# Opening of an attention and token-mixing kernel: which 512 KB tiles the one DMA queue fetches first, and what the first chunks of h wait for

## The chip, the cores and the metric

One core of a Trainium2 chip runs the whole kernel in one launch. The metric is the device time of the launch in microseconds (us), the median of several runs. Times inside the kernel come from one profiled execution and are counted from the start of its span. TensorE is called PE, VectorE DVE, ScalarE ACT, GpSimd POOL, and SyncE, which issues almost all the DMAs here, SP.

## The reference

The input `x` has 2048 tokens of 1024 channels. A modulation vector is made from one condition row, two residual blocks follow:

```
mod = (silu(c) @ w_mod) split in six rows sa, ca, ga, sb, cb, gb   # 1024 each
h   = layernorm(x) * (1 + ca) + sa
x   = x + ga * attention(h)       # 32 heads of 32, four segments of 512 tokens:
                                  # causal softmax inside a segment, plus a linear memory over the earlier ones
h   = layernorm(x) * (1 + cb) + sb
x   = x + gb * mixer(h)           # MLP across the 2048 tokens, 3584 wide, gelu
```

What matters here is the beginning: the scale row `1 + ca` and the shift row `sa` are needed before the first h exists, and h of the first segment (512 tokens) before any query, key or value.

## The kernel before

All matrix products of the large stages are made from two-part operands: a value is split into a rounded high part (ACT or DVE casts it) and a low part (the difference, by DVE or POOL), `split` at L118, and three products high-high, high-low, low-high are summed. In the opening, everything passes through these steps:

- **Loads.** One queue, on SP, issues tile loads of 512 KB in program order: four scale tiles (`fetch_scale(0)`, L309; tiles `wms0` to `wms3`), the four token tiles `x0` to `x3` of the first segment (L310), four more scale tiles (`fetch_scale(1)`, L311), then, inside the loop of L332, eight shift tiles `wm0` to `wm7`, with the three weight parts of head group 0 (v part 0, q part 0, v part 1) behind the first three. The tiles `wms` and `wm` share eleven buffers.
- **Scale.** The row `ca` is made in two halves of 512 channels. `scale_row(cb)` (L293) multiplies the silu of the condition, one column for each of eight steps, with four loaded tiles and adds up one row in PSUM; `scale_columns(cb, ...)` (L301) copies the row, turns it into four columns by PE, one per chunk of 128 channels, and adds 1. The first half serves chunks 0 to 3, the second chunks 4 to 7.
- **Shift.** Here the weights lie transposed, so a DVE instruction (L335) multiplies a tile `wm` of chunk ct with the broadcast condition `scb` and sums along the row: one column of `sa` per chunk.
- **Normalization.** `norm_all` (L214) takes statistics of the four token tiles on DVE, a few tiny steps, and then normalizes two tiles on ACT (L236) and two on DVE (L234).
- **Chunks of h.** For each of eight chunks, `h_chunk` (L244) has PE transpose four blocks (L247, into one of two PSUM banks), ACT apply scale and shift (L249), ACT cast the high part and DVE make the low part. `first_chunk` (L315) then multiplies the chunk with the weights of head group 0 into three PSUM banks: twelve products for key and value (L195), three for the query (L203).

After chunk 7 the second segment's token tiles are treated in the same way (`seg_load(1)`, `seg_chunks`, with the high part on DVE and every second low part on POOL), the first group's keys, values and queries are copied out of PSUM by ACT (L401, L402, L407) and stacked by small DMAs into operands for the scores. Then 32 iterations of attention run: two passes, eight head groups, two segments each. At the beginning of the second pass the pages of h are loaded anew from DRAM (`reload_h`, L360). During the attention, 32 tiles of the other modulation rows are loaded (`mod_fetch`, L572) into the same three buffers as the raw weights. Behind it come the output projection and the mixer, whose products are made by a seven-product recursion.

Who comes first on an engine is not written out by hand. A scheduler walks through the program, keeps a simulated clock for each engine and the queue, and places, of the instructions whose inputs would be ready, the one that stands first in the program (those under `tc.high_priority()`, as in `scale_row` and `norm_all`, before others). The result is a fixed order for each engine, in which every instruction waits for its own inputs and all behind it wait with it. `tc.issue_after(i)` adds one constraint: what is under it is placed after `i`. In the kernel before, `h_chunk` stands under `tc.issue_after` of the second scale row's last product (L337). A change in the opening can so change the order of later instructions as well.

Of the kernel before, what the change touches and what calls it, by code (L numbers as in the profile page):

```python
# [7 lines left out]
F32 = mybir.dt.float32  # L8
# [4 lines left out]
ALU = mybir.AluOpType  # L13
# [4 lines left out]
S, D, H, DH, F = 2048, 1024, 32, 32, 3584  # L18
P = 128
# [25 lines left out]
def attention_and_mlp(ctx, tc, x, wq, wkv, wo, beta, w1, b1, w2, b2, c, wm_a, wm_b, out):  # L45
    nc = tc.nc
    V, A, G, T, SY = nc.vector, nc.scalar, nc.gpsimd, nc.tensor, nc.sync
# [18 lines left out]
    scb, gaw = (a.tile([P, D], F32, name=n) for n in ("scb", "gaw"))  # L66
# [8 lines left out]
    def bank(tag, bufs, name):  # L75
        return psum.tile([P, 512], F32, tag=tag, bufs=bufs, name=name)
# [35 lines left out]
    saca = acst.tile([P, NK, 2], F32, name="saca")  # L112
# [5 lines left out]
    def split(dst, src, hi_eng, lo_eng):  # L118

        hi, lo = dst[:, 0], dst[:, 1]  # L120
        if hi_eng is A:
            last_hi[0] = A.copy(hi, src)  # L122
        else:
            hi_eng.tensor_copy(hi, src)
        return lo_eng.tensor_tensor(lo, src, hi.bitcast(F32), op=ALU.subtract)  # L125
# [18 lines left out]
    def new_page(name):  # L144
        return page.tile([P, 2, 512], F32R, tag="page", bufs=16, name=name)
# [5 lines left out]
    def fetch_part(g, kind, part):  # L151
        r = a.tile([P, D], F32, tag="raw", bufs=3, name=f"raw{kind}{g}_{part}")
        SY.dma_start(r, (wkv if kind == "v" else wq)[g, :, 1024 * part:1024 * part + 1024])
        return r

    def split_part(g, kind, part, r):

        for i in range(2):
            w = aw.tile([P, 2, 512], F32R, tag="w", bufs=8, name=f"w{kind}0_{g}_{part}_{i}")
            split(w, r[:, 512 * i:512 * i + 512], A, V)  # L160
            W[0, g][kind, 2 * part + i] = w

    def load_part(g, pr, kind, part, res):

        if pr == 0:
            split_part(g, kind, part, fetch_part(g, kind, part))
            return
        for i in range(2):
            w = aw.tile([P, 2, 512], F32R, tag="w", bufs=8, name=f"w{kind}{pr}_{g}_{part}_{i}")
            SY.dma_start(w.bitcast(F32), wsp[g, 2 * part + i if kind == "v" else 4 + i])  # L170
            res[kind, 2 * part + i] = w
# [13 lines left out]
    W = {}  # L185
# [23 lines left out]
    def load_x(pool, tt):  # L209
        t = pool.tile([P, D], F32, tag="x", bufs=XB, name=f"x{tt}")  # L210
        SY.dma_start(t, x[P * tt:P * tt + P])
        return t

    def norm_all(tiles):  # L214

        with tc.high_priority():
            flat = csb.rearrange("p a k -> p (a k)")
            r, t = flat[:, 8:12], flat[:, 12:16]
            nb = t
            mv = flat[:, 0:8].rearrange("p (i a) -> p i a", a=2)  # L220
            for k, src in enumerate(tiles):
                st = const.tile([P, 2, 6], F32, tag="st", bufs=4, name="st")
                for i in range(2):
                    V.bn_stats(st[:, i], src[:, 512 * i:512 * i + 512])
                last_stats = V.bn_aggr(mv[:, k], st)
            A.activation(r, mv[:, :, 1], AF.Ln, bias=eps)
            exp = A.activation(r, r, AF.Exp, scale=-0.5)
            V.scalar_tensor_tensor(t, mv[:, :, 1], EPS, r, op0=ALU.add, op1=ALU.mult)
            V.scalar_tensor_tensor(t, t, -0.5, r, op0=ALU.mult, op1=ALU.mult)
            V.scalar_tensor_tensor(r, t, 1.5, r, op0=ALU.add, op1=ALU.mult)  # L230
            V.scalar_tensor_tensor(nb, mv[:, :, 0], -1.0, r, op0=ALU.mult, op1=ALU.mult)
            for k, src in enumerate(tiles):
                if k % 2:
                    last_v = V.tensor_scalar(src, src, r[:, k:k + 1], nb[:, k:k + 1], op0=ALU.mult, op1=ALU.add)  # L234
                else:
                    last_a = A.activation(src, src, AF.Identity, scale=r[:, k:k + 1], bias=nb[:, k:k + 1])  # L236
        return last_stats, exp, last_a, last_v
# [6 lines left out]
    def h_chunk(pool, xs, seg, ct):  # L244
        ps = bank(*(("s1", 2), ("s2", 2))[ct % 2] if seg else ("s2", 2), f"hps{seg}_{ct}")
        for i in range(4):
            T.transpose(ps[:, 128 * i:128 * i + 128], xs[i][:, P * ct:P * ct + P], ident)  # L247
        h32 = pool.tile([P, L], F32, tag="h32", bufs=HB, name=f"h32_{seg}_{ct}")
        act = A.activation(h32, ps, AF.Identity, scale=saca[:, ct, 1:2], bias=saca[:, ct, 0:1])  # L249
        pg = new_page(f"h{seg}_{ct}")  # L250
        lo = split(pg, h32, V if seg else A, V if ct % 2 or not seg else G)
        hpages[seg, ct] = pg
        return act, lo
# [26 lines left out]
    s1p = left.__enter__()  # L280
    scale_wm = []

    def fetch_scale(cb):
        for i in range(4 * cb, 4 * cb + 4):
            t = s1p.tile([P, 2, 512], F32, tag="wm", bufs=11, name=f"wms{i}")
            SY.dma_start(t.rearrange("p a n -> p (a n)"), wm_a[1, i])
            scale_wm.append(t)
# [5 lines left out]
    def scale_row(cb):  # L293
        ps = bank(*(("ms", 1), ("s1", 2))[cb], f"srow{cb}")
        with tc.high_priority():
            for k in range(NK):
                mm = T.matmul(ps[0:1], sc[:, k:k + 1], scale_wm[4 * cb + k // 2][:, k % 2], start=(k == 0),
                              stop=(k == NK - 1))
        return ps, mm

    def scale_columns(cb, ps):  # L301
# [4 lines left out]
                     skip_group_check=True)  # L306
        V.tensor_scalar_add(saca[:, 4 * cb:4 * cb + 4, 1], scale_ps[:, 4 * cb:4 * cb + 4], 1.0)

    fetch_scale(0)  # L309
    xs = {0: [load_x(s1p, tt) for tt in range(4)]}  # L310
    fetch_scale(1)  # L311
    W[0, 0] = {}
    first = [bank("pj", 2, "nps0_0"), bank("pj", 2, "nps0_1"), bank("s1", 2, "qps0")]

    def first_chunk(ct):  # L315
        h = hpages[0, ct]
        for half in range(2):
            kv_chunk(W[0, 0], h, half, ct, two_tiles(first[half]))
        q_chunk(W[0, 0], h, ct, first[2])

    srow = [scale_row(0)]
    V.tensor_copy(bc, sc.unsqueeze(2).to_broadcast([P, NK, P]))
    for i in range(2):
# [1 line left out]
        for j in range(4):  # L325
            T.transpose(ps[:, 128 * j:128 * j + 128], bc[:, 4 * i + j], ident)
        A.copy(scb[:, 512 * i:512 * i + 512], ps)
    last_stats = norm_all(xs[0])[0]
    srow.append(scale_row(1))
    for cb in range(2):  # L330
        scale_columns(cb, srow[cb][0])
    for ct in range(NK):  # L332
        wm = s1p.tile([P, D], F32, tag="wm", bufs=11, name=f"wm{ct}")
        last_wm = SY.dma_start(wm, wm_a[0, ct])
        V.scalar_tensor_tensor(wm, wm, 1.0, scb, op0=ALU.mult, op1=ALU.mult, accum_out=saca[:, ct, 0:1])  # L335
        if ct < 3:
            load_part(0, 0, *(("v", 0), ("q", 0), ("v", 1))[ct], W[0, 0])  # L337
        with tc.issue_after(srow[1][1].ins):
            h_chunk(s1p, xs[0], 0, ct)
        if ct:  # L340
            first_chunk(ct - 1)
    first_chunk(NK - 1)
# [261 lines left out]
    def seg_load(seg):  # L604
        seg_x[seg] = [load_x(s2p, tt) for tt in range(4 * seg, 4 * seg + 4)]
        return norm_all(seg_x[seg])
# [9 lines left out]
    with tc.issue_after(last_wm.ins):  # L616
        _, exp, _, normed_v = seg_load(1)
# [73 lines left out]
    for n in range(-LEADS, 4 * NI + VL):  # L691
# [11 lines left out]
        if 59 <= m < 67:  # L703
            seg, ct = 2 + (m - 59) // 4, 2 * ((m - 59) % 4)
# [146 lines left out]
    for products, tt in (((0, 1), 0), ((2,), 1), ((3, 4, 8), 8), ((9,), 9), ((10,), 2), ((11,), 10), ((12,), 3),  # L851
# [5 lines left out]
        for i in products:  # L857
            if i > 1:
                f = product(i)
# [283 lines left out]
```

## Time and profile before

| what | us |
|---|---|
| median of three runs | 2238.1 |
| the three runs | 2237.97 to 2238.53 |
| the profiled execution | 2237.2 |
| its span, first to last instruction | 2235.5 |
| PE busy in the span | 2194.0 |
| DVE, ACT, POOL busy | 1678.2, 1136.2, 731.9 |

The time of the profiled execution is its span and 1.7 us around it. Lines of a timeline give start, duration, engine, source line, operation, output<-input tiles, shapes and a count of merged instructions; in brackets stands how long the engine was idle before, and what ended that wait. A matmul's duration is longer than the time for which it occupies PE, since matmuls overlap. Lines of a table of windows give the window, its length, the busy time of PE, PE's weight loads, DVE, ACT and POOL with the number of instructions in brackets, the granted PE clock (1.00 is full), the share of the DMA engines that was busy, and GB/s. `SPq` lines are the queue: an issue's start is when SP was free to issue it.

### The profile page before, as it was taken

What the parts mean: (1) busy time and instruction counts of PE and PEld (TensorE: products, weight loads), DVE (VectorE), ACT (ScalarE), POOL (GpSimd) and SP (SyncE); (2) the same over time, 40 slices, a digit from 0 to 9 for tenths busy, and PEclk for the clock granted to TensorE, in tenths of its full rate; (3) what the DMA queues carried; (4) which work ended last, traced back from release to release, by engine and by line L of the source; (5) the groups of instructions that cost most, each with busy time, mean ns of one, the idle gap of its engine ahead of it and who ended that gap; (6) DMA issues with size and microseconds to landing.
All of it is one profiled execution on the core that took longest, in us unless ns stands there. A gap on an engine that the chain in (4) does not pass through costs nothing.

```text
span 2235.5 us, 38277 instructions
## 1 busy us (share of the span) xinstructions
PE 2194.0 (98%) x13786; PEld 1883.5 (84%) x13786; DVE 1678.2 (75%) x3762; ACT 1136.2 (51%) x2082; POOL 731.9 (33%) x831
## 2 busy tenths in 40 slices
PE   8999999998999999999999999999999999999999
PEld 5989898887999899888888888888888888888887
DVE  7677677766777777655758766888888886969687
ACT  5477777665666666655546633533334242424232
POOL 2176666656777676654001200033330000000000
PEclk9999999999999999999999999999999999999999
DMA  7656665687566566665664587655556541414134
GB/s 284 192 175 205 170 180 168 179 299 230 163 194 194 162 197 185 195 192 181 226 205 161 222 328 261 251 212 222 206 201 232 204 144 59 153 57 146 57 123 151
DMA packets 175185, 423.05 MB, mean 189 GB/s; under 512 B 17524, under 2 KB 71828, under 8 KB 166036
## 3 DMA queue, kind: packets, MB, share of 16 engines
q1 hardware_dynamic: 174996, 420.61, 57.2%
q8 instruction: 109, 1.79, 0.3%
q14 instruction: 80, 0.66, 0.1%
HBM read 244.62 MB, written 125.06 MB: 165 GB/s over the span
## 4 chain that ended last, share of the span: by engine, by line
PE 84%; POOL 4%; DMA 3%; ACT 3%; DVE 3%; issue 2%; SPq 1%; ACTq 0%; DVEq 0%; POOLq 0%
PE mx L923 48%; PE nps L195 11%; PE po L793 8%; PE qps L203 6%; PE pv L549 3%; POOL ph L535 2%; PE a L520 1%; PE sz L484 1%; ACT ph L533 1%; DMA sk<-nt 1%; PE sx L484 1%; DVE wv L125 1%; POOL p L531 1%; PE a L523 1%; PE up L466 1%
## 5 line engine op out<-in xcount | busy, mean ns | idle before, releaser
L923 PE MATMUL mx<-bU,sp 128*128 128x512 f32 x2352 | 534.2, 389 | 0.9 <-DVE ac L930 0.9
L923 PEld LDWEIGHTS mx<-bU,sp 128*128 128x128 f32 x2352 | 441.1, 188 | 93.5 <-issue 1.3
L195 PE MATMUL nps<-wv,h 128*128 128x256 f32 x3072 | 437.9, 282 | 1.8 <-POOL h L125 0.7
L535 POOL TENSOR_TENSOR ph<-p,ph 128x640 f16<-128x640 f32 x256 | 383.6, 1520 | 156.1 <-ACT ph L533 153.3
L122 ACT CAST sp<-wr 128x384 fp32r<-128x384 f32 (+2 forms) x408 | 217.0, 545 | 426.7 <-PE mx L923 347.3
L923 PE MATMUL mx<-bA,sp 128*128 128x512 f32 x1764 | 430.5, 389 | 0.0
L195 PEld LDWEIGHTS nps<-wv,h 128*128 128x128 f32 x3072 | 404.6, 189 | 9.9 <-DVE h L125 2.0
L923 PEld LDWEIGHTS mx<-bA,sp 128*128 128x128 f32 x1764 | 331.1, 188 | 68.8
L125 DVE TENSOR_TENSOR sp<-wr,sp 128x384 fp32r<-128x384 f32 (+2 forms) x408 | 260.5, 650 | 31.1 <-ACT sp L122 30.8
L930 DVE TENSOR_TENSOR ac<-mx,ac 128x512 f32<-128x512 f32 x280 | 190.3, 688 | 85.1 <-PE mx L923 84.4
L203 PE MATMUL qps<-h,wq 128*128 128x512 f32 x768 | 198.3, 399 | 0.2
L533 ACT CAST ph<-p 128x1280 f16<-128x1280 f32 x128 | 161.3, 1260 | 44.4 <-POOL p L531 43.7
L793 PE MATMUL po<-wo,ots 128*128 128x512 f32 x768 | 179.3, 390 | 0.0
L793 PEld LDWEIGHTS po<-wo,ots 128*128 128x128 f32 x768 | 143.3, 188 | 29.0 <-DVE x L796 0.2
L923 PE MATMUL mx<-bB,sp 128*128 128x512 f32 x588 | 164.0, 389 | 0.0
L203 PEld LDWEIGHTS qps<-h,wq 128*128 128x128 f32 x768 | 140.7, 189 | 27.5 <-ACT vp L407 0.9
L531 POOL TENSOR_SCALAR_AFFINE_SELECT p<-p 128x256 f32<-128x256 f32 x256 | 121.9, 487 | 99.2 <-ACT p L528 52.4
L549 PE MATMUL pv<-vp,ph 128*128 128x97 bf16 (+1 forms) x2560 | 143.8, 203 | 3.0 <-DVE red L556 1.5
L549 PEld LDWEIGHTS <-ph 128*128 128x128 f16 x2560 | 115.8, 99 | 26.6 <-issue 11.5
L486 DVE CUSTOM_DVE_ANT_0 sx<-sx,mask 128x128 f32<-128x128 f32 (+1 forms) x256 | 93.8, 366 | 49.3 <-PE sx L484 47.4
L923 PEld LDWEIGHTS mx<-bB,sp 128*128 128x128 f32 x588 | 110.3, 188 | 22.9
L930 DVE TENSOR_TENSOR cc<-mx,cc 128x512 f32<-128x512 f32 x140 | 95.0, 685 | 39.6 <-PE mx L923 39.6
(207 smaller groups left out, 3165.7 us busy)
## 6 DMA issues: line engine op xcount, KB each, us to landing
sk<-sg SPq DMA_DIRECT2D x384, 128.0 KB
wr<-in_w_dram SPq DMA_DIRECT2D x28, 1024.0 KB
wr<-in_w_dram SPq DMA_DIRECT2D x32, 768.0 KB
bstu<-ucd SPq DMA_DIRECT2D x28, 768.0 KB
wsp<-wv SPq DMA_DIRECT2D x32, 512.0 KB
rawm<-in_wm_b_dram SPq DMA_DIRECT2D x32, 512.0 KB
wv<-wsp SPq DMA_DIRECT2D x32, 512.0 KB
pcd<-cc SPq DMA_DIRECT2D x14, 1024.0 KB
```

What stands on the lines that cost most here:

```text
L122: last_hi[0] = A.copy(hi, src)
L125: return lo_eng.tensor_tensor(lo, src, hi.bitcast(F32), op=ALU.subtract)
L195: T.matmul(ps[:, aa], h[:, j, 128 * tt:128 * tt + 128], wt[:, i, o:o + 256], start=(n == 0), stop=(n >= 6 * NK - 2), skip_group_check=True)
L203: T.matmul(ps, wt[:, i, o:o + 128], h[:, j], start=(k + n == 0), stop=(3 * k + n == 3 * NK - 1))
L486: marks[4 * t + h - LEADS, "V"] = V.tensor_tensor_reduce(o, o, mask[:, 384 - 128 * i:], 1.0, -3.0e38, op0=ALU.add, op1=ALU.max, accum_out= ...
L531: G.affine_select(w, w, pattern=[[0, 2], [1, 128]], compare_op=ALU.is_ge, fill=0.0, base=0, channel_multiplier=-1)
L533: marks[n, "A"] = A.copy(ph[:, 0], p32)
L535: marks[n, "G"] = G.tensor_tensor(ph[:, 1, c], p32[:, c], ph[:, 0, c], op=ALU.subtract)
L549: T.matmul(pv[:, i, 0:w], ph[:, part, o:o + 128], d["vp"][:, j, h, 0:w], start=(n == 0), stop=(n == 19), skip_group_check=True)
L793: T.matmul(ps, os_[:, i, P * ct:P * ct + P], wop[ct, nh][:, j], start=(n == 0), stop=(n == 3 * NK - 1))
L923: T.matmul(ps, ops[q][:, i, P * k:P * k + P], b[:, j], start=(m == 0 and first), stop=(m == 3 * nk - 1), skip_group_check=True)
L930: V.tensor_tensor(d, ps, d, op=ALU.add)
```

## The change

The loads of the opening are put in another order, and the constraints on what follows are exchanged:

- The loads `wm0`, v part 0, `wm1`, q part 0 and `wm2` are issued after the token tiles and ahead of the second scale half's tiles `wms4` to `wms7`; v part 1 comes behind those. `wm3` to `wm7` stay in the loop.
- The fetch of a weight part and its split, until now one call (`load_part`), are two calls.
- `h_chunk` is no longer under the constraint on the second scale row's last product.
- Instead the shift sums are placed after the normalization's last DVE instruction, and the weight splits after its last ACT and DVE instruction.

```diff
+    W[0, 0] = {}
+    shift_wm = []
+
+    def fetch_shift(ct):
+        wm = s1p.tile([P, D], F32, tag="wm", bufs=11, name=f"wm{ct}")
+        shift_wm.append((wm, SY.dma_start(wm, wm_a[0, ct])))
+
     fetch_scale(0)
     xs = {0: [load_x(s1p, tt) for tt in range(4)]}
+    first_parts = (("v", 0), ("q", 0), ("v", 1))
+    first_raw = []
+    for ct in range(3):
+        fetch_shift(ct)
+        if ct < 2:
+            first_raw.append(fetch_part(0, *first_parts[ct]))
     fetch_scale(1)
-    W[0, 0] = {}
+    first_raw.append(fetch_part(0, *first_parts[2]))
...
-    last_stats = norm_all(xs[0])[0]
+    last_stats, _, first_a, first_v = norm_all(xs[0])
     srow.append(scale_row(1))
     for cb in range(2):
         scale_columns(cb, srow[cb][0])
     for ct in range(NK):
-        wm = s1p.tile([P, D], F32, tag="wm", bufs=11, name=f"wm{ct}")
-        last_wm = SY.dma_start(wm, wm_a[0, ct])
-        V.scalar_tensor_tensor(wm, wm, 1.0, scb, op0=ALU.mult, op1=ALU.mult, accum_out=saca[:, ct, 0:1])
+        if ct > 2:
+            fetch_shift(ct)
+        wm, last_wm = shift_wm[ct]
+        with tc.issue_after(first_v.ins):
+            V.scalar_tensor_tensor(wm, wm, 1.0, scb, op0=ALU.mult, op1=ALU.mult, accum_out=saca[:, ct, 0:1])
         if ct < 3:
-            load_part(0, 0, *(("v", 0), ("q", 0), ("v", 1))[ct], W[0, 0])
-        with tc.issue_after(srow[1][1].ins):
-            h_chunk(s1p, xs[0], 0, ct)
+            with tc.issue_after(first_a.ins), tc.issue_after(first_v.ins):
+                split_part(0, *first_parts[ct], first_raw[ct])
+        h_chunk(s1p, xs[0], 0, ct)
         if ct:
             first_chunk(ct - 1)
```

## Prediction

> **What bounds the kernel now.** I read the page's head and the stage table first: where does TensorE (PE) lose time, and in which stage does the change lie?
>
> ```profile
> span 2235.5 us, 38277 instructions
> PE 84%; POOL 4%; DMA 3%; ACT 3%; DVE 3%; issue 2%; SPq 1%; ACTq 0%; DVEq 0%; POOLq 0%
> 0.00:61.64 61.64, 51.99 (x282) 33.99 (x282) 44.25 (x91) 31.48 (x54) 15.15 (x50) 0.97 0.74 275
> 61.64:1060.00 998.36, 971.18 (x8342) 881.20 (x8343) 705.40 (x2062) 645.19 (x1175) 617.25 (x718) 0.99 0.64 192
> ```
>
> PE is 84% of the chain that ended last. In the two stretches (columns: length, busy PE, PE load, DVE, ACT, POOL, clock, DMA share, GB/s) it idles 9.7 us up to 61.64 us, where it begins the second segment's long run of products, and 27.2 us in the attention after it. The change lies in the first stretch. Next the DMA queue of the opening:
>
> ```profile
> 10.81 0.33 SPq L334 DMA_DIRECT2D wm<-in_wm_a_dram  x1
> 15.93 0.33 SPq L334 DMA_DIRECT2D wm<-in_wm_a_dram  x1
> 24.88 4.18 SPq L211 DMA_DIRECT2D x<-in_x_dram  x4
> ```
>
> Each issue waits for the transfer eight places ahead, so an issue's start is that one's landing: x0 at 10.81, wms4 at 15.93 (four places after x0, (15.93-10.81)/4 = 1.28 us per 512 KB tile), wq0 at 24.88. One tile per 1.28 us is the pace of the whole opening. Then the engines there:
>
> ```profile
> 5.80 3.52 PE L297 MATMUL srow<-wms,sc 128*1 128x512 f32 x4 [5.80 <-DVE sc L110]
> 10.28 5.31 PE L297 MATMUL srow<-wms,sc 128*1 128x512 f32 x12
> 15.96 1.88 PE L297 MATMUL srow<-wms,sc 128*1 128x512 f32 x4 [0.37 <-DMA wms<-in_wm_a_dram]
> 17.77 1.05 PE L305 MATMUL scale<-ident,MZ 1*128 1x1 f32 x8
> 17.98 2.38 ACT L236 ACTIVATE x<-x,csb 128x1024 f32<-128x1024 f32 x2 [0.82 <-DVE csb L231]
> 18.75 5.31 PE L297 MATMUL srow<-wms,sc 128*1 128x512 f32 x12
> 22.34 1.14 ACT L122 CAST wv<-rawv 128x512 fp32r<-128x512 f32 x2 [1.98 <-DMA rawv<-in_wkv_dram]
> 24.68 0.78 ACT L249 ACTIVATE h<-hps,saca 128x512 f32<-128x512 f32 x1 [1.21 <-PE hps L247]
> 26.40 0.72 PE L195 MATMUL nps<-wv,h 128*128 128x256 f32 x4
> 33.02 0.68 DVE L125 TENSOR_TENSOR h<-h,h 128x512 fp32r<-128x512 f32 x1
> 33.62 1.20 DVE L335 SCALAR_TENSOR_TENSOR wm<-wm,scb 128x1024 f32<-128x1024 f32 x1
> 43.60 1.11 PE L195 MATMUL nps<-wv,h 128*128 128x256 f32 x8
> 45.71 1.11 PE L195 MATMUL nps<-wv,h 128*128 128x256 f32 x8
> 46.66 0.63 PE L203 MATMUL qps<-h,wq 128*128 128x512 f32 x2
> 36.54 0.44 PE hps L247 x4
> ```
>
> From 10.28 PE hardly stops: first scale row, second row (15.96 to 24.06), then h's transposes and the first group's products, ending at 47.29. The first product waits for the second row, but PE is working on that row meanwhile. (The last row is from the chain: four transposes cost PE 0.44; one chunk's products cost 45.71-43.60 = 2.11.)
>
> **The change, part by part.** *Queue.* Five tiles (wm0, v0, wm1, q0, wm2) go ahead of wms4 to wms7. By the pace they land at 15.93 to 21.06 instead of 21.06 to 26.2, and the second row's tiles at 22.34 to 26.2 instead of 15.93 to 19.8. The other v part and all later loads keep their places. Twenty issues before, twenty after: no cost. wm7 now reuses wm0's buffer, read by DVE at about 20.8, ahead of its turn at 23.6: none.
>
> *Waits.* h chunks no longer stand behind the second row; the new waits put shift sums and weight splits behind the normalization of x, where both engines' built order had them already: none. In the changed program's built order ACT does x0, x2, the four weight casts, and only then the first two h chunks; PE's third chunk of transposes needs the bank that the first of these frees. ACT: 17.98+2.38+2x1.14+0.78 = 23.4. So PE has from 15.6 to 23.4 only half of the scale columns (0.5) and eight transposes (2x0.44): over 6 us empty where before it did most of the second row. **That row's work isn't removed, it moves behind.** Ahead of the first product then stand two groups of transposes and one of the row's four tiles (4x5.31/12 = 1.77): 23.4+0.88+1.77 = 26.1 at full clock, against 26.40.
>
> *PE's ledger from 23.4.* Six transpose groups 6x0.44 = 2.6; second row (12+4)x5.31/12 = 7.1; its columns 0.5; eight chunks 8x2.11 = 16.9; six transposes of the next segment, which the built order puts before the last chunk's end, 0.7. Sum 27.8, so 51.2 at full clock. DVE needs 1.20 for a shift sum and 0.68 for a low part per chunk, under 2.11, and three of the sums and three weight parts are done before PE starts, so I add no waits. Then the clock:
>
> ```profile
> 47.00:50.00 3.00, 1.24 (x8) 0.65 (x7) 2.75 (x7) 3.00 (x8) 0.00 (x0) 1.00 0.01 3
> 50.00:53.20 3.20, 3.18 (x16) 2.50 (x15) 0.54 (x2) 2.42 (x4) 0.28 (x1) 0.52 0.02 5
> 53.20:56.00 2.80, 2.76 (x19) 2.25 (x18) 2.77 (x4) 2.80 (x7) 1.02 (x1) 0.94 0.21 41
> 424.00:428.00 4.00, 2.77 (x32) 2.41 (x30) 4.00 (x9) 3.80 (x12) 3.51 (x4) 1.00 0.40 163
> ```
>
> With PE 1.24 busy in 3 us, the granted clock was 0.52 in the next 3.2; with 1.2 us empty in 4 it stayed 1.00. The changed opening is emptier than the first case, so I take half clock for 3.5 us of work from 23.4 (the kernel's own start shows the same: row records take 3.52/4 = 0.88 there, 0.44 from 10.28). Loss 1.75 (bounds 0 and 3.5). The first group's products end near **52.9, 5.6 later** than 47.29.
>
> *The handover gives most of it back.*
>
> ```profile
> 46.84 0.35 ACT L401 COPY k<-nps 128x256 f32<-128x256 f32 x1
> 48.14 0.43 ACT L407 CAST vp<-nps 128x256 bf16<-128x256 f32 x1
> 48.41 2.42 ACT L236 ACTIVATE x<-x,csb 128x1024 f32<-128x1024 f32 x2
> 51.61 1.45 ACT L249 ACTIVATE h<-hps,saca 128x512 f32<-128x512 f32 x2 [0.78 <-PE hps L247]
> 52.95 0.58 ACT L122 CAST sg<-kps 128x512 fp32r<-128x512 f32 x1
> 53.89 0.66 ACT L434 ACTIVATE rk<-k 128x512 f32<-128x512 f32 x1
> 54.42 0.65 ACT L443 CAST vp<-r 128x512 bf16<-128x512 f32 x1
> 54.93 1.16 ACT L122 CAST wv<-rawv 128x512 fp32r<-128x512 f32 x2
> 58.15 0.76 DVE L124 CAST h<-h 128x512 fp32r<-128x512 f32 x2
> 58.65 4.20 POOL L125 TENSOR_TENSOR h<-h,h 128x512 fp32r<-128x512 f32 x2 [4.43 <-DVE h L124]
> 61.64 8.02 PE L195 MATMUL nps<-wv,h 128*128 128x256 f32 x68 [0.69 <-POOL h L125]
> ```
>
> Before, after the last product come six ACT copies (46.84 to 48.57), the next x's normalization and its transposes at half clock; h follows at 51.61. In the changed order that normalization stands ahead of the copies, beside PE's products, and so do transposes. The copies begin when the first half's products end, 0.9 before 52.9, plus 0.2: 52.2, end 53.9, and h follows at once: 2.3 later than 51.61, not 5.6. Then ACT's order: two h chunks 1.45, cast 0.6, rk 0.66, two weight casts 1.16, cast 0.58, vp 0.65, third h chunk 0.75, and DVE's cast 0.45: 6.3, less some 0.2 of overlap, so the third chunk's high part is ready at 60.0 against 58.57 (first of the two casts at 58.15). POOL's low part and PE's restart follow as before, 61.64-58.57 = 3.05 later (bounds: 2.1, the mean of POOL's two pieces, and 4.2, both of them). 63.05 against 61.64: **the opening costs +1.4** (+0.5 to +2.6; -0.3 without the clock's loss). PE's work left from there is the same in both built orders.
>
> *The rest.* The scheduler reorders the attention too (PE's orders agree again only near 1060 us; after that nothing moves). That has no row. Bounds: the 27.2 us of idle there could shrink by its largest wait, below, or grow by another such; I take 0, since PE's products ahead of each iteration's first one, counted at their rows' durations, agree in both orders mostly within 2 us.
>
> *Sum:* the profiled execution took 2237.2 (span 2235.5 and 1.7 around it); 2237.2 + 1.4 = 2238.6. The median of the runs shown is 0.9 above that execution: **2239.5**.
>
> **The rivals.** *The clock stays full* in the opening: -1.75, so 2237.8. [...] The rows from 47.00 speak against it: the clock fell although PE was empty for only 1.8 us there.
>
> *Slower: the switch of passes.*
>
> ```profile
> 490.00:495.00 5.00, 4.67 (x28) 3.81 (x27) 2.06 (x5) 2.64 (x5) 0.52 (x1) 1.00 0.43 100
> 509.48 0.56 SPq L379 DMA_DIRECT2D sk<-sg  x1
> 519.54 0.76 PE L484 MATMUL sx<-sk 96*128 96x128 f32 x2 [6.85 <-DMA sk<-sg]
> ```
>
> At 512.7 PE stands 6.85 us: the last stacked piece, issued at 509.48 behind the reload of h, lands at 519.4. In the changed queue order two modulation tiles move to between the two reloads and a third, with two more pieces, ahead of that last piece: 3x1.28 + 2x0.6 = 5 us. For it: the DMA engines limit that stretch. Against: they were only 0.43 busy at 490 to 495, where two of the tiles may fit, which is where it decides. 2239.5 + 5 = 2244.5.
>
> *Faster: the same wait goes*, because those two tiles no longer stand ahead of the first reload (2x1.28 earlier) and by the built order PE has some 1.4 us more products before it: at most -6.85 and the half clock behind it (some 1.75), so 2239.5 - 8.6 = 2230.9; half of that is 2235.2, so it decides only if most of the wait goes.
>
> *It doesn't do what it says:* later chunks still need the second row's columns, and if PE meets them late nothing moves: 2238.1.
>
> **How the numbers follow.** Forecast 0.36, full clock 0.12, no effect 0.04: all within 0.2% (4.5 us, about what a measurement of this kernel tells from no change), 0.52 in all. Slower switch, or a like stall elsewhere: 0.29. Faster: 0.19. The range 2232 to 2247 reaches into the faster case and beyond the slower one by the 2 us that the iterations' work differs; it leaves out the 0.1 of a faster case in full and 0.1 of larger stalls. The forecast's own range is 2235 to 2243.
>
> **What would show it.** wms4 landing at 22.3; PE mostly empty from 15.6 to 23.4, then granted near 0.5 for some 3.5 us; last first-group product near 52.9 with no wait over 0.5 behind 27; h of the second segment at 53.9; PE's long run from 63 (61.64 before). Wrong if that run starts before 61 or after 65, or if the time comes from behind 61.64: then the reordering, not the opening, decides, and the wait at 512.7 is where I look first.

## The result and the profile after

| | before | changed |
|---|---|---|
| median, us | 2237.97 (2233.97 to 2242.01, 7 runs) | 2246.62 (2240.86 to 2252.19, 7 runs) |
| ratio | | 1.0046, 95% interval 1.0035 to 1.0057 |
| profiled execution, its span, us | 2237.2, 2235.5 | 2243.91, 2242.2 |
| granted clock, mean over the span | 0.995 | 0.992 |

The change costs some 10 us (0.0046 of 2238; the medians lie 8.65 apart). The profiled execution is one of the faster ones of the changed kernel and shows 6.7 of them. They are there before the mixer begins, and nothing moves behind that. The first product of the mixer, from the timeline of before and then from that of the changed kernel:

```profile
1163.83 2.20 PE L923 MATMUL mx<-bA,sp 128*128 128x512 f32 x9
```

```profile
1170.34 1.98 PE L938 MATMUL mx<-bA,sp 128*128 128x512 f32 x8
```

It starts 6.5 us later, and the span ends 6.7 later. So the opening or the attention lost them. The opening first; PE's timeline and one row of the queue in the changed kernel (lines behind L320 are 15 higher than before's):

```profile
17.64 1.05 PE L305 MATMUL scale<-ident,MZ 1*128 1x1 f32 x8 [0.77 <-DVE MZ L303]
20.71 0.66 PE L247 MATMUL hps<-ident,x 128*128 128x128 f32 x4 [0.47 <-ACT x L236]
23.45 1.11 PE L247 MATMUL hps<-ident,x 128*128 128x128 f32 x4 [2.09 <-ACT h L249]
24.50 3.57 PE L297 MATMUL srow<-wms,sc 128*1 128x512 f32 x4
28.76 0.72 PE L195 MATMUL nps<-wv,h 128*128 128x256 f32 x4
18.77 5.43 SPq L314 DMA_DIRECT2D wm<-in_wm_a_dram  x5
```

PE waits for ACT's first h chunk until 23.45 and only then does the second scale row; the four records that took 5.31/3 = 1.77 us in before take 3.57. The windows show why (clock is the third number from the end):

```profile
21.00:23.40 2.40, 0.36 (x4) 0.13 (x2) 2.40 (x7) 2.40 (x6) 0.00 (x0) 0.70 1.03 410
23.40:27.00 3.60, 3.55 (x7) 1.05 (x8) 3.60 (x7) 3.09 (x5) 0.00 (x0) 0.50 1.04 412
27.00:30.00 3.00, 3.00 (x12) 1.49 (x11) 2.21 (x4) 1.14 (x2) 0.00 (x0) 0.70 1.02 410
```

The handover to the second segment, from the timeline of the same kernel:

```profile
54.46 0.62 PE L203 MATMUL qps<-h,wq 128*128 128x512 f32 x2
55.79 1.50 ACT L249 ACTIVATE h<-hps,saca 128x512 f32<-128x512 f32 x2
62.39 0.42 DVE L124 CAST h<-h 128x512 fp32r<-128x512 f32 x1
62.89 2.02 POOL L125 TENSOR_TENSOR h<-h,h 128x512 fp32r<-128x512 f32 x1 [4.43 <-DVE h L124]
65.89 1.31 PE L195 MATMUL nps<-wv,h 128*128 128x256 f32 x10
```

The first group ends at 55.08, 7.8 later than before, and the long run starts at 65.89, 4.25 later. The wait at the switch of passes did not grow, it is 6.36 us against 6.85:

```profile
527.00 0.80 PE L499 MATMUL sx<-sk 96*128 96x128 f32 x2 [6.36 <-DMA sk<-sg]
```

The other place lies where the prediction did not look. Queue, DVE, PE and two windows of the changed kernel about 842 us:

```profile
837.54 0.59 SPq L589 DMA_DIRECT2D rawm<-in_wm_b_dram  x1
838.80 0.16 DVE L473 TENSOR_SCALAR rdd<-rd 128x8 f32<-128x8 f32 x1
842.00 1.23 DVE L593 SCALAR_TENSOR_TENSOR rawm<-rawm,scb 128x1024 f32<-128x1024 f32 x1 [3.04 <-DMA rawm<-in_wm_b_dram]
843.39 0.42 DVE L475 TENSOR_TENSOR am<-rd,rdd 128x256 f32<-128x256 f32 x1
843.96 1.51 PE L481 MATMUL up<-v,pk 128*128 128x132 f32 x8 [1.90 <-DVE am L475]
840.00:844.00 4.00, 2.10 (x30) 1.98 (x28) 1.77 (x4) 2.14 (x3) 2.63 (x5) 1.00 0.99 312
844.00:848.00 4.00, 4.00 (x23) 3.93 (x24) 1.32 (x4) 1.70 (x4) 3.50 (x8) 0.57 1.02 381
```

and the load and the sum of the same modulation tile (29 of 0 to 31) in before:

```profile
822.34 0.38 SPq L574 DMA_DIRECT2D rawm<-in_wm_b_dram  x1
835.03 1.89 DVE L578 SCALAR_TENSOR_TENSOR rawm<-rawm,scb 128x1024 f32<-128x1024 f32 x1
```

In before the load is issued at 822.34, and DVE's sum finds its tile there. In the changed kernel the scheduler put the load on SP behind 15 small DMAs, nine stacking pieces, four rows of maxima and two stores; it is issued at 837.54 and lands at 842.0. DVE's order has the sum between two steps that make `am`. DVE stands 3.04 us, `am` comes late, PE stands 1.90 us ahead of the memory update `up`, and of the four us from 844 it runs at 0.57 of its clock (1.7 us lost).

**Theory before the experiments:** the opening costs what its trace shows, some 4 us, and the rest is the reordered attention. The rivals are: the opening costs all of it; or any reordering costs as much, since before's order is well tuned; or particular waits make an order dear.

### The profile page after: what moved, and what is told of

Its sections match the earlier page's. It is cut to its first block, busy times and chain, and to the rows that moved or that the text cites. A ratio compares the mean times of both kernels' runs of the same rounds, so it can differ in the third digit from the quotient of the medians.

```text
span 2242.2 us, 38292 instructions
## 1 busy us (share of the span) xinstructions
PE 2200.2 (98%) x13786; PEld 1886.2 (84%) x13786; DVE 1684.5 (75%) x3762; ACT 1133.2 (51%) x2082; POOL 729.8 (33%) x831
## 4 chain that ended last, share of the span: by engine, by line
PE 85%; DMA 5%; DVE 4%; ACT 2%; POOL 2%; issue 2%; SPq 1%; ACTq 0%; DVEq 0%; POOLq 0%
PE mx L938 46%; PE nps L195 11%; PE qps L203 7%; PE po L808 6%; PE pv L564 3%; POOL ph L550 1%; PE a L535 1%; PE sz L499 1%; PE sx L499 1%; PE srow L297 1%; DMA rawm<-in_wm_b_dram 1%; PE a L538 1%; PE up L481 1%; PE sy L499 1%; DMA h<-hT 1%
```

## Experiments

Most of them take the opening and the attention apart. After the program is traced, the instructions from the attention's loop on are chained, engine by engine, in a given order that was recorded from another kernel's program. All instructions and semaphores stay as they are, so a kernel can have one opening and another's order. Lines move by a few (L578 is L582 in these kernels with before's opening). The kernels hold the given orders as packed numbers, so the diffs of orders here are written in short. The edit, here for the changed opening with before's order:

```diff
+    for e, given in ORDER.items():
+        for a, b in zip(given, given[1:]):
+            tc.add_manual_dep(traced[e][b], traced[e][a].name, NO_SYNC, reason="given order")
```

| kernel | median, us (runs) | ratio to before, 95% interval |
|---|---|---|
| e1 changed opening, before's order | 2240.66 (11) | 1.0009 [1.0000, 1.0019] |
| e2 before's opening, changed order | 2245.95 (6) | 1.0034 [1.0022, 1.0046] |
| e3 loads moved, h still held, before's order | 2241.99 (8) | 1.0022 [1.0011, 1.0033] |
| e4 h not held, old loads, before's order | 2237.95 (11) | 1.0000 [0.9992, 1.0009] |
| e5 changed order in the first pass | 2239.83 (11) | 1.0008 [0.9999, 1.0016] |
| e6 changed order in the second pass | 2243.52 (12) | 1.0023 [1.0014, 1.0033] |
| e7 a third order | 2246.04 (5) | 1.0031 [1.0019, 1.0043] |
| e8 e1 with seven idle products | 2241.09 (11) | 1.0017 [1.0009, 1.0026] |
| e9 a fourth order | 2236.61 (11) | 0.9998 [0.9989, 1.0007] |
| e10 e1 with three idle products | 2239.37 (11) | 1.0007 [0.9998, 1.0016] |
| e11 e2, tile 29's load early | 2240.28 (12) | 1.0012 [1.0002, 1.0021] |
| e12 before, tile 23's load early | 2238.41 (11) | 1.0003 [0.9994, 1.0011] |
| e13 changed kernel, tile 29's load early | 2243.24 (7) | 1.0030 [1.0018, 1.0041] |
| e14 before, tile 29's load late | 2241.21 (11) | 1.0021 [1.0012, 1.0029] |

Before ran beside each group (e1 to e4, e5 to e8, e9 and e10, e11 to e14), with medians of 2237.64, 2237.63, 2237.74 and 2237.61.

### Opening or order

> The changed opening, and behind it, from the attention's loop on, the order of before on every engine. Theory (two parts add up: the opening's delay of 4.2 us, as the restart of the second segment's products moved from 61.64 to 65.89 us, is carried through, and the reordered attention adds the rest): +4.2 us against before, 1.0019. Rival, all in the opening: +10, 1.0046. Rival, all in the reordering, the opening's delay is absorbed where the attention waits for other things: within 1 us, 1.0000.

> The opening of before, and behind it, from the attention's loop on, the order of the changed kernel on every engine. Theory: what is left of +10.3 without the opening's 4.2, so +6 us, 1.0027 (the two profiled executions alone would give +2.4, 1.0011). Rival, all in the opening: 1.0000. Rival, all in the reordering: +10, 1.0046.

e2 is before's kernel with the given order of the changed one. The opening alone costs +2.0 us (interval 0 to 4.2), the order alone +7.6 (4.9 to 10.3); 1.0009 and 1.0034 make 1.0043, against 1.0046 for the whole. So the two add up, and the reordered attention is some three quarters of the loss, by the middle of wide intervals. The opening seems worth less in time than the 4.25 us of its trace, which lie at the upper end of its interval.

### The two halves of the opening

> One half of the change alone: the new order of loads, with h's chunks still held behind the second scale row, and the attention in the order of before. Theory (the second row's tiles land 6.4 us later, PE stands empty before them and then runs at half clock): PE starts that row at 22.5, needs 7.1 us and about 2.9 for the half clock, then eight chunks in 20.4 us: restart of the second segment's products near 64 to 66, +3 to +4.5 us. Rival (the harm comes from letting h's chunks go first, which puts the row's products between them): within 1 us of before.

```diff
-        h_chunk(s1p, xs[0], 0, ct)
+        with tc.issue_after(srow[1][1].ins):
+            h_chunk(s1p, xs[0], 0, ct)
```

> The other half alone: the loads in the order of before, but h's chunks not held behind the second scale row, and the attention in the order of before. Theory (the row's tiles are there from 15.93 us, so PE has work and keeps its clock): within 1 us of before, 0.9995 to 1.0005. Rival (freeing h's chunks is what harms): +3 to +4.5 us.

```diff
-        with tc.issue_after(srow[1][1].ins):
-            h_chunk(s1p, xs[0], 0, ct)
+        h_chunk(s1p, xs[0], 0, ct)
```

The loads moved alone cost +4.4 us by the medians (ratio 1.0022); h not held alone changes nothing (1.0000); both together are e1's +2.0 by the ratio and +3.0 by the medians. So the moved loads do the harm, since the second scale row gets its tiles 5 x 1.28 us later. That freeing h takes part of it back is not shown: the intervals of e3 and e1 overlap.

### Is the opening's loss the clock?

> The changed opening with before's order for the attention (earlier 2240.66 us, ratio 1.0009) and seven products without use on PE, 2 behind the first scale columns, 1 and 4 behind the first chunks' transposes, in the time in which PE was empty (18.6 to 19.5 us, 20.1 to 20.6 us, 21.4 to 23.3 us). Clock theory: PE loses 2.9 us there because it runs at half clock from 21.9 to 28.8 us after having been empty; filled, it stays at full clock, the first product of the first chunk starts at about 25.5 us and not 28.2 us, and the time falls by 2 to 3 us: 2238 us, ratio 0.9996 to 1.0000. Rival: the opening's end is set by tiles and by ACT's and DVE's work and not by PE's clock: the first product starts earlier and the restart behind the first group stays, 2240 to 2241 us. If the half clock is there in spite of the filling, the empty time is not its cause.

```diff
+    def idle_work(behind, count):
+        fills[behind.ins.name] = [
+            T.matmul(srow[0][0][0:1], sc[:, 0:1], bc[:, 0:4].rearrange("p a n -> p (a n)"), start=True, stop=True).ins
+            for _ in range(count)]
...
```

These products (added work that nothing reads) took 0.9 us each and not 0.45, so seven of them filled more time than was empty: the half clock was gone, but the third chunk's transposes came at 25.61 and the first product at 28.41, as late as at half clock. This run tells little. With three:

> As the run with the filled empty time, but with three products without use in place of seven, since each took 0.9 us and not 0.45: one behind the first scale columns (0.9 of 1.1 us empty) and two behind the second chunk's transposes (1.8 of 1.9 us empty). Clock theory: full clock through 30 us, the third chunk's transposes start at 23.3 us as without filling, the first product at 26 us and not 28.2 us, the restart behind the first group 2 us earlier: 2238 to 2239 us, ratio 0.9995 to 1.0003. Rival (the opening's end is set by tiles, ACT and DVE): the first product comes earlier, the restart does not, 2240 to 2241 us, ratio 1.001. If the half clock comes back although PE is empty for less than 1 us in all, it does not hang on this empty time.

PE's timeline and the window of e10:

```profile
23.25 0.66 PE L258 MATMUL hps<-ident,x 128*128 128x128 f32 x4 [0.28 <-ACT h L262]
26.05 0.71 PE L199 MATMUL nps<-wv,h 128*128 128x256 f32 x4
60.14 2.02 POOL L129 TENSOR_TENSOR h<-h,h 128x512 fp32r<-128x512 f32 x1 [4.43 <-DVE h L128]
23.40:27.00 3.60, 3.60 (x18) 1.63 (x18) 3.60 (x7) 2.88 (x5) 0.00 (x0) 1.00 1.02 406
```

The clock stays full, the first product starts at 26.05 (28.24 in e1), and POOL's low part of the third chunk at 60.14 (62.33 in e1): 2.2 us come back at both places, so here it was PE's empty time that brought the half clock. The traces bear it out: in the changed kernel's the clock stands at half from 21.96 to 28.79, for 6.83 us, and e10's windows from 18 to 34 stand at 1.00 throughout. Four records of the second row take 3.57 us in the changed kernel and 3.51 in e1, with nothing filled, and 1.88 in e8 and e10; in e3 its sixteen take 8.60 us where full clock takes 7.1. The rival "the end of the opening hangs on something else" falls for the trace. In time e10 is 1.3 us below e1, which these intervals do not tell apart.

### Which part of the order, and is it any order?

> Before's opening; the attention's first pass (iterations 0 to 15) in the changed kernel's order on every engine, from the 17th iteration on before's order. In the run with the changed order throughout, the loss was +7.6 us (ratio 1.0034). Theory 'first pass': that order loses PE's time at a few places of the first pass (its profile has a 10.2 us stretch at half clock about 124 to 134 us, where before's has none): 2243 to 2245 us, ratio 1.0025 to 1.0034. Theory 'second pass' (its profile goes from +1.7 us at iteration 26 to +6.2 us at iteration 27): 2238 to 2240 us, ratio 1.000 to 1.001. If the loss is spread evenly, half of it: about 2241.5 us, 1.0017.

> The counterpart: before's opening and before's order through the first pass, the changed kernel's order from the 17th iteration on. Theory 'first pass': 2238 to 2239 us, ratio 1.000 to 1.0005. Theory 'second pass': 2243 to 2245 us, ratio 1.0025 to 1.0034. Spread evenly: about 2241.5 us. The two halves together should give about the +7.6 us of the whole; if they don't, the switch between the orders matters.

The edit of e5: up to the first transposed key of iteration 16 the instructions stand in the changed order, behind it those that are left stand in before's; e6 the other way.

```diff
-given = before
+given = changed[:k] + [i for i in before if i not in changed[:k]]
```

+2.2 us and +5.9: they add up to the whole within their intervals, and most lies in the second pass. "First pass", for which the 10 us at half clock about 124 us spoke, falls. An even spread, 1.0017 each, lies just above e5's interval and inside e6's.

> Before's opening; for the attention a third order, the one that the scheduler finds when only the first shift tile and v part 0 are fetched ahead of the second scale row's tiles. It differs from before's order at 5670 of 13214 places on PE, from the changed one at 6385. Theory 'this order': the changed order is unlucky and another costs nothing in particular: 2236 to 2240 us, ratio 0.999 to 1.001. Theory 'tuned order': before's order is better than what a reshuffle gives in general, so the third order loses about as much as the changed one: 2242 to 2248 us, ratio 1.002 to 1.0045.

> Before's opening; for the attention a fourth order, which the scheduler finds when v part 0 and q part 0 are fetched ahead of the second scale row's tiles and the shift tiles behind them. It differs from before's order at 6931 of 13214 places on PE, from the changed one at 6401, from the third at 6588. Theory 'before's order is better than a reshuffle in general' (the changed order cost +7.6 us, the third +8.4 us): 2241 to 2248 us, ratio 1.0015 to 1.0045. Theory 'two bad draws': within 2 us of before, ratio 0.999 to 1.001, or faster.

```diff
-given = before
+given = third
```

(e9: `fourth`.) The third costs as much as the changed one, the fourth nothing, though half of its places on PE differ from before's. So "any reordering costs" falls too: an order is dear or not by what is in it. The traces of these kernels show one thing that goes with it, DVE's wait between the load and the sum of modulation tile 29. The third order:

```profile
839.43 0.58 SPq L578 DMA_DIRECT2D rawm<-in_wm_b_dram  x1
844.22 1.23 DVE L582 SCALAR_TENSOR_TENSOR rawm<-rawm,scb 128x1024 f32<-128x1024 f32 x1 [2.46 <-DMA rawm<-in_wm_b_dram]
844.00:848.00 4.00, 3.87 (x42) 3.71 (x39) 3.46 (x10) 1.29 (x3) 3.58 (x3) 1.00 1.01 331
675.23 1.14 PE L470 MATMUL up<-v,pk 128*128 128x132 f32 x8 [1.46 <-DVE pv L556]
```

The fourth:

```profile
820.86 0.34 SPq L578 DMA_DIRECT2D rawm<-in_wm_b_dram  x1
831.12 1.28 DVE L582 SCALAR_TENSOR_TENSOR rawm<-rawm,scb 128x1024 f32<-128x1024 f32 x1
```

Both dear orders issue the load near 838 or 839 and let DVE stand (the third also 3.23 us for tile 17 at 672); both cheap ones issue it near 821 or 822. A wait of DVE is not yet one of PE, though: in the third order PE has other products, is busy for 3.87 of the four us from 844 and keeps its clock, and only behind tile 17 it stands 1.46 us, at 675. So tile 29's wait costs the third order nothing in this trace, and what makes that order dear is not shown. The wait in e2, the changed order behind before's opening:

```profile
838.26 0.58 SPq L578 DMA_DIRECT2D rawm<-in_wm_b_dram  x1
843.05 1.93 DVE L582 SCALAR_TENSOR_TENSOR rawm<-rawm,scb 128x1024 f32<-128x1024 f32 x1 [4.12 <-DMA rawm<-in_wm_b_dram]
845.71 1.14 PE L470 MATMUL up<-v,pk 128*128 128x132 f32 x8 [3.67 <-DVE am L464]
844.00:848.00 4.00, 2.29 (x19) 2.31 (x20) 2.50 (x8) 1.12 (x4) 2.98 (x4) 0.90 1.01 391
848.00:852.00 4.00, 4.00 (x38) 3.81 (x38) 1.96 (x8) 1.66 (x6) 1.19 (x3) 0.67 0.96 375
```

In e6, which has the changed order in the second pass alone, DVE stands 3.37 us for the same tile and PE 2.22, at full clock throughout (844 to 848: 1.00):

```profile
845.60 1.14 PE L470 MATMUL up<-v,pk 128*128 128x132 f32 x8 [2.22 <-DVE am L464]
```

### One DMA moved

> Before's opening and the changed order (2245.95 us, ratio 1.0034), with one DMA moved: the load of modulation tile 29 is issued right behind the store ahead of the 15 stacking DMAs, as in before's order, and not behind them. Theory 'late load': DVE's wait of 4.1 us about 842 us goes, with it PE's 3.7 us at the memory update and the half clock that follows (1.7 us): 2240.5 to 2242.5 us, ratio 1.0012 to 1.0022. Rival 'many small waits': this one is made up for by the slack further on, 2244.5 to 2246 us, ratio 1.003 or above.

The edit is in SP's given order alone:

```diff
 oT    <- ot23
+rawm29 <- wm_b
 sk0_0 <- sg26
...
 sk0_2 <- sg26
-rawm29 <- wm_b
 sk0_3 <- sg26
```

In e11's trace the wait is gone:

```profile
819.77 0.38 SPq L578 DMA_DIRECT2D rawm<-in_wm_b_dram  x1
833.59 1.83 DVE L582 SCALAR_TENSOR_TENSOR rawm<-rawm,scb 128x1024 f32<-128x1024 f32 x1
```

The median falls from 2245.95 to 2240.28, by 5.7 us; PE's 3.67 in e2 and 1.7 of half clock (the 0.10 and 0.33 that the two windows from 844 lack, of four us each) make 5.4. The same move in the changed kernel itself:

> The changed kernel as it is (its opening and its order, 2246.62 us, ratio 1.0046), with the same single DMA moved as in the first of these runs. Theory 'late load': 2241.5 to 2244 us, ratio 1.0018 to 1.003: what is left is the opening's +2 us and a part of the reordering that hangs on other waits. Rival 'many small waits': 2245.5 to 2247 us, ratio 1.0037 to 1.0046.

2246.62 falls to 2243.24, by 3.4 us; in the changed kernel's trace PE's 1.90 and 1.7 of half clock make 3.6. By itself this pair would not show it, since the two intervals (1.0035 to 1.0057 and 1.0018 to 1.0041) overlap. The reverse, in before:

> The kernel before with one DMA moved the other way: the load of modulation tile 29 is issued behind the 15 stacking DMAs, as in the changed order. DVE's sum of this tile starts at 835 us in before, and the load would land at about 841 us. Theory 'late load': DVE waits about 6 us, PE about 3 us and then runs 3.4 us at half clock: 2241 to 2243.5 us, ratio 1.0015 to 1.0027. Rival 'many small waits': 2237 to 2239 us, ratio 1.000 to 1.0006.

```diff
 oT    <- ot23
-rawm29 <- wm_b
 sk0_0 <- sg26
...
 sk0_2 <- sg26
+rawm29 <- wm_b
 sk0_3 <- sg26
```

```profile
840.29 1.94 DVE L582 SCALAR_TENSOR_TENSOR rawm<-rawm,scb 128x1024 f32<-128x1024 f32 x1 [5.08 <-DMA rawm<-in_wm_b_dram]
843.16 1.90 PE L470 MATMUL up<-v,pk 128*128 128x132 f32 x8 [2.99 <-DVE am L464]
840.00:844.00 4.00, 1.01 (x7) 0.87 (x6) 3.67 (x10) 0.00 (x0) 1.15 (x1) 0.92 1.00 349
844.00:848.00 4.00, 4.00 (x36) 3.64 (x36) 1.97 (x9) 1.44 (x5) 1.73 (x5) 0.65 1.04 398
```

One DMA issued behind 15 others, with all else as in before, makes before 3.6 us slower (ratio 1.0021, interval 1.0012 to 1.0029), and the same chain is there: DVE, `up`, half clock. Of the three medians e14's lies inside the range of "late load", e13's in its upper half and e11's 0.2 us below it; none is near the rival's, though e13's interval reaches into that. Last, the wait of the same kind that before itself has:

> The kernel before with one DMA moved: the load of modulation tile 23 is issued 14 places earlier, right behind the store, at about 734 us and not 745.7 us. Theory 'late load': DVE's wait of 3.4 us at 750 us goes, with it PE's 2.6 us behind it and a half clock of 3.4 us that follows: 2233.5 to 2236 us, ratio 0.9982 to 0.9993. Rival: no difference, 2237 to 2238 us.

```diff
 oT    <- ot20
+rawm23 <- wm_b
...
 sk1_2 <- sg23
-rawm23 <- wm_b
 sk1_3 <- sg23
```

Here the theory failed. In before DVE stood 3.44 us for tile 23, and PE waited twice behind it:

```profile
750.50 1.23 DVE L578 SCALAR_TENSOR_TENSOR rawm<-rawm,scb 128x1024 f32<-128x1024 f32 x1 [3.44 <-DMA rawm<-in_wm_b_dram]
752.05 0.91 PE L549 MATMUL pv<-vp,ph 128*128 128x97 bf16 x20 [0.89 <-DVE red L556]
756.36 0.51 PE L520 MATMUL a<-sk 98*128 98x512 f32 x1 [1.71 <-DMA sk<-nt]
```

In e12 DVE's wait is gone, and PE has one wait in place of two, of about the same sum:

```profile
749.18 1.50 DVE L582 SCALAR_TENSOR_TENSOR rawm<-rawm,scb 128x1024 f32<-128x1024 f32 x1
758.60 0.77 PE L524 MATMUL a<-sk 98*128 98x512 f32 x1 [2.70 <-DMA sk<-nt]
```

PE then waits for the stacked rows of maxima, which come by DMA; by the trace they were late by as much in any case, and DVE's wait cost nothing beside theirs. No version came out that beats before beyond what the runs tell.

## Why the prediction was wrong

The forecast was 2239.5, and the sum of its terms 2238.6: the opening +1.4, the attention 0.

**The step that failed** is "The rest": "I take 0, since PE's products ahead of each iteration's first one, counted at their rows' durations, agree in both orders mostly within 2 us." Measured, the reordering costs +7.6 us (e2). That PE's work stands in nearly the same places says nothing of when the other engines' inputs arrive. One load that moved on SP, against a sum that did not move with it on DVE, makes some 3.4 to 5.7 us of it (e13, e11; 3.6 in the other direction, e14). The built orders of SP and DVE, set beside each other, show the load 15 places later and the sum, as in before's order, ahead of the step that makes `am`; I compared PE's alone.

**The bound beside it was close:** "or grow by another such" wait, 6.85, falls 0.75 short of the 7.6, whose interval it lies in. The slower rival named the mechanism, tiles of the modulation that move on the queue and stand ahead of or behind small pieces, but at the wrong place: the switch of passes kept its wait (6.36 us), and its "like stall elsewhere" is what came. The faster rival, by which that wait goes, fails with the same row. The closing sentence of the prediction, that the long run's start after 65 us or time from behind means that the reordering decides, held.

**The opening's steps**, against the changed kernel's trace:

| step | forecast | measured |
|---|---|---|
| landing of wms4 | 22.3 | 22.6 (the eighth issue behind it, fourth of five from 18.77 in steps of 1.28) |
| third chunk's transposes | 23.4 | 23.45 |
| loss by the clock | 1.75 (0 to 3.5) | 2.8, by the windows' clock: 3.55 x 0.5 + 3.00 x 0.3 + 0.36 x 0.3 = 2.8 |
| PE's ledger from there, full clock | 27.8 | 29.1 (e10, from 23.25 to 52.3) |
| last first-group product | 52.9 | 55.08 |
| second segment's h | 53.9 | 55.79 |
| third chunk's high part | 60.0 | 62.81 |
| long run | 63.05 | 65.89 |
| the opening, in time | +1.4 (0.5 to 2.6) | +2.0 (0 to 4.2), e1 |

The mechanism held up to the handover. Too small were the clock's loss (half clock held for 6.83 us, from 21.96 to 28.79, where I took 3.5) and the ledger, in which the second row's columns stood at 0.5 though one half's columns take 1.05 (the other 0.75 us of its 1.3 are not accounted for). The handover's last step left out DVE: it takes 7.02 us from 55.79 to 62.81 where the prediction has 6.1, since ACT has the third chunk's h at 61.01 and DVE, at work on low parts, casts it only at 62.39. The first two make 2.2 of the 2.8 us by which the long run came later than forecast, this step 0.9, and the copies took 0.3 less. Two slips change nothing: there are 23 tile issues on either side and not twenty, and 61.64 - 58.57 is 3.07. That e10 removes the clock's loss and moves the restart's low part from 62.33 to 60.14 shows that it was the clock. The rival "the clock stays full" is wrong for this opening, and e10 shows what it would have been worth: its first product starts at 26.05, against the 26.1 of the forecast's full-clock figure.

**What stays open:** with tile 29's load early the changed kernel is still at 1.0030, some 6.7 us above before. The opening is +2.0 of it, the first pass's order +2.2 (e5, whose interval reaches to 0); no single wait was found for that, nor for the 2 to 3 us that are left, nor for the third order's loss. Part of it may be clock and not waits. From 61.64 to 1060 PE stood 25.4 us in the changed kernel's trace against 27.2 in before's, but by the clock records 27.3 us of that stretch ran at half clock, against 17.1 in before. The longest piece is 10.24 us from 127.8 on, and the last section shows that such a piece comes and goes without the order. Over all runs the mean clock averaged 0.9948 in before (105 runs), 0.9943 in e2, 0.9927 in the changed kernel and 0.9924 in the third order. Whether an order brings more half clock, beyond what follows tile 29's wait, no run here separates.

## What to carry to other kernels

An edit in one stage that goes through a scheduler is an edit of every later stage, and the untouched part can cost several times the edited one (here 7.6 us against 2.0). Before calling a reordering free, compare the orders of the queue and of each consumer, and look for a load that moved behind a train of small DMAs while its consumer kept its place in a full engine's order. A given order, recorded from the old kernel, separates the two effects in two runs, and moving one DMA in it both ways shows a cause where a trace only suggests one; that the same wait was free in another place (e12) says that each has to be tried.

## What the runs showed of the hardware

Half clock came in pieces of three lengths. In before's trace, whose clock record begins at 9.15, they last 3.41 us from 50.11, 6.83 from 244.67, 6.83 from 517.73 and 3.41 from 756.66; in the changed kernel's, whose record begins at 11.72, 6.83 from 21.96, 10.24 from 127.78, 3.41 from 284.79, 3.41 from 431.56, 6.83 from 523.72 and 3.41 from 844.58. Each record has one more piece at its end, which the end cuts. What PE did ahead of a fall differs. In the changed kernel's opening the clock fell at about 22.0 (the window from 21.00 at 0.70 has 1.44 us of half clock, up to its end at 23.40). By then PE had waited 0.89, 0.47 and 0.6 us (the beginning of the 2.09), with two groups of transposes of 0.66 us between. In e2 the clock fell where PE was busy nearly all the time by its records (3.08 of the 3.40 us up to 124.50), in the score products about 124 us:

```profile
121.10:124.50 3.40, 3.08 (x19) 1.84 (x16) 3.37 (x14) 3.40 (x7) 0.96 (x1) 0.86 0.37 79
124.50:127.90 3.40, 3.40 (x25) 2.48 (x22) 1.98 (x8) 2.05 (x4) 3.40 (x4) 0.50 0.66 157
```

Before, with nearly the same products in the same order, and less busy (2.83 of the 3.40 us from 124.50, against 3.40), stays at full clock there:

```profile
121.10:124.50 3.40, 3.08 (x20) 1.72 (x19) 3.37 (x16) 3.40 (x7) 1.32 (x1) 1.00 0.25 54
124.50:127.90 3.40, 2.83 (x21) 1.83 (x21) 2.80 (x10) 2.99 (x8) 3.40 (x4) 1.00 0.76 217
```

It is not the order that decides there. Up to the one load that it moves (738.65 in its trace) e12 has before's opening and order, and its execution falls to half clock at the same products:

```profile
121.10:124.50 3.40, 3.07 (x19) 1.83 (x16) 3.40 (x14) 3.40 (x7) 0.98 (x1) 0.87 0.37 79
124.50:127.90 3.40, 3.40 (x24) 2.44 (x21) 1.94 (x8) 2.07 (x4) 3.40 (x4) 0.50 0.61 161
```

So this stretch comes and goes with the execution, and no run here shows what decides it. The clock also goes with the spread between runs of one program: of before's 105 runs beside these kernels, the 6 with a mean clock of 0.993 took 2239.9 us on average, the 8 with 0.997 took 2235.4. All 105 lie between 2232.05 and 2242.36, so a single profile can be some 5 us off either way, which is why the order's cost had to be found by medians and not by comparing two traces.
